# Rooms of two banks for the whole kernel: one PSUM pool, a gather with one eviction, taps in two transfers, and a new order of a gated mix of two long convolutions

## The chip, the cores and the metric
The kernel runs on one core of a Trainium2 chip. The metric is the device time of one launch in microseconds (us). The kernel before takes 266.55 us, the median of three runs from 265.99 to 267.28. On the core, TensorE (PE) multiplies matrices, with PEld for its weight loads; VectorE (DVE), ScalarE (ACT) and GpSimd (POOL) work on elements; SyncE (SP) issues most transfers, and ACT and POOL have DMA queues of their own. Matmuls write into PSUM, which this kernel divides into eight banks of 512 fp32 columns by 128 partitions; ACT or DVE copies or multiplies a result out of it ("evicts" it), and then its place is taken by another.

## The reference: what is computed
Length L is 2048, D is 448 channels, N is 256 complex modes per channel, and everything is bf16 from outside. Two long convolutions along the sequence are mixed by a gate.

```python
x = A_u                                             # [1, 2048, 448]
g = sigmoid((x * gate_w).sum(-1, keepdims=True))
# a: S4. A kernel made of 256 modes per channel, then a causal convolution
dt = exp(log_dt); logdA = dt * (A_re + 1j*A_im); dB = dt * (B_re + 1j*B_im)
K = einsum("dn,dnl,dn->dl", C, exp(logdA[:, :, None] * l), dB).real
a = irfft(rfft(u, 2L) * rfft(K, 2L))[:L] + u * Dskip
# b: H3. Four shifted taps of k, times v, a causal convolution, times q (here q = x)
kv = sum_t(k shifted by t * shift_k[:, ks - 1 - t]) * v
b = x * (irfft(rfft(kv, 2L) * rfft(ssm_k, 2L))[:L] + kv * ssm_D)
return g * a + (1 - g) * b
```

## The kernel before, in words
**Transforms as matmuls.** The 448 channels are cut into four column groups of 28 columns for each of the four partition groups (`NQG`, `NC`). Each convolution of a column group goes through the same stages, each a set of matmuls into PSUM and an eviction back to SBUF: `spread` (L328, PSUM tile `ps_c`, result `zs`), `transform` (`ps_2`, named `ps` in some rows), a product of two spectra on DVE (`products`), `stage_a` (`ps_a`, result `U`) and `stage_b` (`ps_b`, whose result is multiplied or copied into `ug` or `uu`). The "B" convolutions (H3) take the columns of `vt` and of `ssm_k`; the "A" convolutions (S4) take those of `uu` and of a kernel that has to be made first.

**Making the S4 kernel.** `Tables` (L555 on) turns the modes into tables of powers `ET` with exponentials and sines on ACT; the phases `ks_ph` and the real parts `ks_mag` come through matmuls that multiply by a diagonal matrix of dt (`ks_dt`) and through DVE. Exponential and sine need different function tables, so ACT loads a table (`ACT_TABLE_LOAD`) where it goes from one to the other. `KGen.block` (L464) does it in eight blocks of 14 columns: DVE builds the tables `kg_TQ`, `kg_P` and `kg_TP`, 224 small matmuls add up in the PSUM tile `pk`, and ACT evicts it as `kg_S`. `KGen.gather` (L511) then picks and shifts the pieces with small matmuls into `ps_g`, in two halves of 448 columns, each evicted with one copy into `kg_KT`; and `block` (L891) spreads these 14 columns into `zsK` (again `ps_c`). Two blocks make one column group.

**PSUM.** Pool `psum` (L722) has three shared rooms of two banks each: all stages take the next free one. Pool `psk` (L723) has two tiles of one bank: `pk` for the accumulation (L885), one buffer for the whole kernel, and `ps_g`, also one buffer, which `gather` takes twice per block and `spread` four times (groups of 4, 4, 4 and 2 columns) in the first six blocks. The spread of the last two blocks goes through shared rooms, in groups of 8 and 6. `evac` (L728) is a copy on ACT; `evac_two` (L731), used in the last block and at the end, alternates between ACT (even index) and DVE (odd).

**The opening.** Before the first spread of `vt`, the H3 input must be there: the four taps of `shift_k` come with four transfers on ACT's queue (L781–782) into `wraw`, DVE multiplies them with unit matrices into `diag` (the row `front<-scratch`, since `diag` lies in the tile `front`, L820–822), PE multiplies the transposed k with them (`ps_v`, L823–833), and DVE multiplies eight such tiles with v in place (`vt<-ps_v,vt`, L834–835). `ks_dt` is made from `ldt` by an exponential and a copy (L815–819).

**The order.** Nothing is issued when it is written. `Order` and `Listed` (L124–155) record each call with its number, and `issue` plays them back in the hand-written list `ORDER` (L42–112), with a dependency from each instruction to the one before it on the same engine. So the list fixes the order on every engine and DMA queue, and a tile's room is claimed in the order of the list too. All instructions show the line of the playback, L149; they are told apart by their tiles.

```python
for run in ORDER.split():
    a, _, b = run.partition("-")
    for f, args, kw in self.calls[int(a):int(b or a) + 1]:
        ins = f(*args, **kw)
```

**The end.** `step` (L955 on) interleaves the stages of one column group with block j of the S4 kernel for the next. After the last block come the half transforms and stages of the last group, whose two halves alternate evictions between ACT and DVE, and 16 output transfers.

Of the kernel before, what the change touches and what calls it, by code (L numbers as in the profile page):

```python
# [136 lines left out]
class Order:  # L137

    def __init__(self, tc):
        self.tc, self.calls = tc, []  # L140
        for e in ("vector", "scalar", "tensor", "gpsimd", "sync"):
            setattr(self, e, Listed(self.calls, getattr(tc.nc, e)))

    def issue(self):
        last, done = {}, 0
        for run in ORDER.split():
# [914 lines left out]
```

## Time and profile before
| | |
|---|---|
| runs | 266.55 us median (265.99 to 267.28, three runs) |
| profiled execution | 266.88 us, with a span of 264.8 us |
| DVE busy | 243.4 us (92%) |
| ACT busy | 226.8 us (86%) |
| PE busy, weight loads | 213.7 us (81%), 194.2 us (73%) |
| mean granted PE clock | 0.942 of full speed |
| HBM traffic | 7.95 MB read, 2.87 MB written |

The span runs from the first to the last instruction of the profiled execution; the time of the launch has 2.08 us more around it. "Busy" is the time in which an engine worked on at least one instruction, so the sum of single durations can be above it. A row of groups gives the engine, the operation, the result and its sources, the shape (partitions x elements, type), how often it occurs, the busy time, the mean duration of one in ns, and the idle time just before these instructions, with what ended most of it. A row of the timeline has the start, the length, and in brackets the idle time before. A row of stretches has the stretch, its length, the busy time (and number of instructions) of PE, PEld, DVE, ACT and POOL, the granted PE clock, the mean busy share of the DMA engines, and GB/s.

### The profile page before, as it was taken

Reading aid. Unit: us, or ns where it says so; the run is one execution under the profiler, and the core shown is the slowest. Engines: PE = TensorE matmul, PEld = TensorE weight load, DVE = VectorE, ACT = ScalarE, POOL = GpSimd, SP = SyncE. Lnnn points to the kernel's source line nnn. Section 1 sums busy time; section 2 is a strip of 40 time slices with the busy share of each in tenths; the row PEclk is TensorE's granted clock in tenths of the full one; section 3 lists DMA queues with packets and bytes.
Section 4 is the critical chain, followed back from the end, with each engine's and each line's share of the span. In section 5 each row is a group of like instructions: output and inputs, shape, how many; then the busy total and the mean of one; then the engine's idle time right before and its main releaser. Section 6 shows DMA issues by size and latency. Waiting matters only on the chain.

```text
span 264.8 us, 12775 instructions
## 1 busy us (share of the span) xinstructions
PE 213.7 (81%) x5786; PEld 194.2 (73%) x5786; DVE 243.4 (92%) x506; ACT 226.8 (86%) x375; POOL 11.8 (4%) x46
## 2 busy tenths in 40 slices
PE   1611849799799999999899898899979998989820
PEld 1501739788688889889788788889969888979720
DVE  6599999899999999999989999989999999989950
ACT  2998789997999999999999999999999999485400
POOL 8000000000000100010100100001000100000000
PEclk9999979999999869999999999999986999999955
DMA  7999669952833702045626230423240360600087
GB/s 153 218 189 192 104 134 203 176 83 32 158 72 72 159 4 57 4 80 119 109 51 141 41 92 2 90 56 73 50 97 2 72 144 2 144 5 2 2 158 122
DMA packets 57077, 24.27 MB, mean 92 GB/s; under 512 B 52032, under 2 KB 54720, under 8 KB 57024
## 3 DMA queue, kind: packets, MB, share of 16 engines
q1 hardware_dynamic: 50752, 19.34, 38.9%
q0 software_dynamic: 1008, 3.21, 6.6%
q10 hardware_dynamic: 5264, 0.92, 2.1%
q8 instruction: 45, 0.74, 1.2%
q14 instruction: 8, 0.07, 0.1%
HBM read 7.95 MB, written 2.87 MB: 41 GB/s over the span
## 4 chain that ended last, share of the span: by engine, by line
DVE 37%; ACT 35%; PE 16%; DMA 4%; issue 3%; SPq 0%; ACTq 0%; DVEq 0%
ACT zs L149 12%; ACT zsK L149 7%; ACT ET L149 6%; DVE kg_P L149 5%; PE ps_v L149 4%; ACT U L149 4%; DVE kg_TQ L149 3%; PE ps_b L149 3%; DVE kg_TP L149 3%; DVE ET L149 3%; PE ps_c L149 3%; DVE zsS L149 3%; DVE vt L149 3%; DVE zs L149 3%; DVE sb_G L149 2%
## 5 line engine op out<-in xcount | busy, mean ns | idle before, releaser
L149 ACT CAST zs<-ps 128x896 bf16<-128x896 f32 x48 | 43.8, 944 | 1.9 <-PE ps L149 1.9
L149 ACT CAST zs<-ps_c 128x1024 bf16<-128x1024 f32 (+1 forms) x48 | 44.0, 976 | 0.5 <-PE ps_c L149 0.4
L149 PEld LDWEIGHTS <-front 128*32 128x32 bf16 (+1 forms) x496 | 19.9, 160 | 27.8 <-issue 17.3
L149 PE MATMUL pk<-kg_TP,kg_TQ 128*32 128x32 bf16 x1792 | 35.4, 241 | 0.9 <-issue 0.7
L149 PEld LDWEIGHTS <-kg_TQ 128*32 128x32 bf16 x1792 | 31.8, 160 | 3.5 <-issue 0.9
L149 PEld LDWEIGHTS <-s_W 128*128 128x128 bf16 x544 | 27.9, 98 | 7.9 <-issue 4.5
L149 PE MATMUL ps_a<-sa_R,zs 128*128 128x128 bf16 x224 | 32.0, 231 | 1.2 <-DVE zs L149 0.7
L149 PE MATMUL ps_b<-U,sb_G 128*128 128x28 bf16 x1024 | 30.8, 178 | 2.6 <-DVE U L149 1.2
L149 ACT CAST U<-ps_a 128x1024 bf16<-128x1024 f32 (+1 forms) x30 | 27.9, 962 | 5.4 <-PE ps_a L149 5.4
L149 PEld LDWEIGHTS <-sb_G 128*128 128x128 bf16 x1024 | 28.7, 98 | 4.7 <-issue 1.9
L149 PE MATMUL ps_v<-front 128*32 128x336 bf16 (+3 forms) x448 | 17.3, 319 | 17.1 <-DVE sb_offs L149 6.9
L149 PE MATMUL ps_a<-sa_R,zsS 128*128 128x128 bf16 x224 | 31.1, 227 | 0.0
L149 PEld LDWEIGHTS <-zs 128*128 128x128 bf16 x224 | 29.0, 150 | 1.9 <-DVE zs L149 0.8
L149 PEld LDWEIGHTS <-zsS 128*128 128x128 bf16 x224 | 29.4, 152 | 0.7 <-DVE zsS L149 0.4
L149 PE MATMUL ps<-zs,s_W 128*128 128x112 bf16 x384 | 27.1, 215 | 3.0 <-ACT zs L149 2.5
L149 DVE TENSOR_TENSOR kg_TP<-kg_TP,ET 128x1792 bf16<-128x1792 bf16 x23 | 24.7, 1083 | 0.5 <-ACT ET L149 0.5
L149 DVE TENSOR_TENSOR kg_TQ<-kg_TQ,ET 128x896 bf16<-128x896 bf16 (+1 forms) x36 | 24.6, 720 | 0.0
L149 ACT ACTIVATE ET<-ks_ph 128x448 bf16<-128x448 int16 x40 | 22.6, 596 | 1.8 <-DVE ks_ph L149 1.7
L149 DVE TENSOR_TENSOR kg_P<-kg_TP,ET 128x1792 bf16<-128x1792 bf16 (+1 forms) x25 | 23.3, 934 | 0.1
L149 ACT ACT_TABLE_LOAD x15 | 19.2, 1283 | 2.0 <-issue 1.8
L149 PE MATMUL ps_c<-Wc,uu 128*64 128x128 bf16 x224 | 18.7, 290 | 0.4 <-ACT zsK L149 0.2
L149 PE MATMUL ps_c<-Wc,vt 128*64 128x128 bf16 x224 | 17.2, 289 | 1.2 <-ACT zs L149 1.2
(101 smaller groups left out, 424.7 us busy)
## 6 DMA issues: line engine op xcount, KB each, us to landing
zsS<-zs SPq DMA_DIRECT2D x16, 448.0 KB, 4.4
kg_TP<-kg_P POOLq DMA_DIRECT2D x7, 448.0 KB, 4.4
vt<-in_B_v_dram SPq DMA_DIRECT2D x4, 448.0 KB, 7.5
skraw<-in_B_ssm_k_dram SPq DMA_DIRECT2D x16, 112.0 KB, 3.4
uu<-in_A_u_dram SPq DMA_DIRECT2D x4, 448.0 KB, 7.1
ks_xf<-xfd SPq DMA_DIRECT2D x3, 336.0 KB, 3.1
out_dram<-vt SPq DMA_DIRECT2D x8, 112.0 KB, 4.4
out_dram<-vt ACTq DMA_DIRECT2D x8, 112.0 KB, 4.6
```

What stands on the lines that cost most here:

```text
L149: ins = f(*args, **kw)
```

## The change
- PSUM becomes one pool with four shared rooms of two banks. `psk` is gone: `pk` takes a shared room per block, of which it uses one bank, and `ps_g` takes one shared room of two banks per block.
- `gather` evicts once: both halves lie in the two banks of its room, and a single copy of 896 columns moves them into `kg_KT`. The copy's order runs through the columns of a tap, so consecutive results are written 128 bytes apart.
- The spread of every block goes through shared rooms in groups of 8 and 6 columns, as the last two blocks did.
- The taps come in two transfers instead of four: one for three groups of channels, and one for the fourth.
- `ORDER` is new from end to end. On ACT's queue both transfers of the taps stand ahead of the first table load; before, one did, and three stood behind an exponential that needs `ldt`. On SP's queue `A_re` is first, and all four transposes of k stand ahead of the four transfers of v; before, one of v was ahead of the last transpose. The order has 9 table loads instead of 15, the six fewer all in the opening.
- A list `TURNED` names 15 calls that change their engine when the list is played: 12 copies go from DVE to ACT and three from ACT to DVE. To ACT go four `kg_TP` copies 224 wide, two `kg_TQ` copies 448 wide, the copy of `gw`, that of dt (112 x 4), `gb`, two half-transform copies `zsK<-ps` 448 wide, and one `U` of 768 columns; to DVE go two `zs` spreads of 512 columns and one `zsK` of 1024.
- With all of it ACT has 372 recorded instructions instead of 390, DVE 498 instead of 508, and PE as many as before. 28 more tiles are claimed from the shared rooms, 213 instead of 185.

```diff
 ORDER = (
...
 )
+TURNED = (
+    "62 945 1091 1481 1503 2118 2948 2970 4623 4661 5088 5818 6522 6540 6604 "
+)
...
+    def turn(self):
+        for i in map(int, TURNED.split()):
+            f, args, kw = self.calls[i]
+            self.calls[i] = (self.tc.nc.vector.tensor_copy if f.__name__ == "copy" else self.tc.nc.scalar.copy, args, kw)
+
     def issue(self):
+        self.turn()
...
-        pt = self.pk[:, 0:448].rearrange("p (n b) -> p n b", b=32)
+        pt = self.psum.tile([P, 2, 512], f32, name="pk", tag="ps")[:, 0, 0:448].rearrange("p (n b) -> p n b", b=32)
...
         for r in range(8):
-            if r % 4 == 0:
-                pt = self.psk.tile([P, 512], f32, name="ps_g")
-            o = pt[:, (r % 4) * 112:(r % 4) * 112 + 112].rearrange("p (b n) -> p b n", b=8)
+            if r == 0:
+                pt = self.psum.tile([P, 2, 512], f32, name="ps_g", tag="ps")
+            o = pt[:, r // 4, (r % 4) * 112:(r % 4) * 112 + 112].rearrange("p (b n) -> p b n", b=8)
...
-            if r % 4 == 3:
-                evac(KT[:].rearrange("p n (b r) -> p n b r", r=8)[:, :, :, r - 3:r + 1], pt[:, 0:448].rearrange("p (r b n) -> p n b r", r=4, b=8), r // 4)
+        evac(KT[:].rearrange("p n (b f r) -> p f r b n", b=8, f=2), pt[:, :, 0:448].rearrange("p f (r b n) -> p f r b n", r=4, b=8))
...
-    psum = ctx.enter_context(tc.tile_pool(name="psum", bufs=3, space=PSUM))
-    psk = ctx.enter_context(tc.tile_pool(name="psk", bufs=1, space=PSUM))
+    psum = ctx.enter_context(tc.tile_pool(name="psum", bufs=4, space=PSUM))
...
-    for g in range(4):
-        nc.scalar.dma_start(wraw[:, g], B_shift_k[top(g):top(g) + P, :])
+    rows = B_shift_k[0:P, :]
+    nc.scalar.dma_start(wraw[:, 0:3], bass.AP(rows.tensor, rows.offset, [[4, P], [448, 3], [1, 4]]))
+    nc.scalar.dma_start(wraw[:, 3], B_shift_k[top(3):top(3) + P, :])
...
-    pk = psk.tile([P, 512], f32, name="pk")
...
-        if j >= NBLK - 2:
-            spread(nc, psum, WcK, KA[H], cols, [range(0, 8), range(8, 14)], ev, at=at)
-        else:
-            spread(nc, psk, WcK, KA[H], cols, [range(0, 4), range(4, 8), range(8, 12), range(12, 14)], evac, 4, "ps_g", at)
+        spread(nc, psum, WcK, KA[H], cols, [range(0, 8), range(8, 14)], ev, at=at)
```

More of the change, by code (lines that the diff above doesn't have):

```diff
@@ L406, with __init__ @@
 class KGen:
-    def __init__(self, tc, nc, pool, pk, psk, cons, sel_d, d4, EQ, EP):
-        self.tc, self.nc, self.pk, self.psk = tc, nc, pk, psk
+    def __init__(self, tc, nc, pool, psum, cons, sel_d, d4, EQ, EP):
+        self.tc, self.nc, self.psum = tc, nc, psum
         self.pool, self.cons, self.sel_d, self.d4, self.EQ, self.EP = pool, cons, sel_d, d4, EQ, EP
@@ L884, in body @@
     V.tensor_scalar(out=sel_d[:], in0=dj[:], scalar1=0.0, scalar2=None, op0=ALU.is_equal)
-    pk = psk.tile([P, 512], f32, name="pk")
-    kg = KGen(tc, nc, kgp, pk, psk, cons, sel_d, d4, EQ, EP)
+    kg = KGen(tc, nc, kgp, psum, cons, sel_d, d4, EQ, EP)
     KA = [None] * NQG
```

136 rows, old and new, of the table ORDER are left out of this document.

## The prediction
> **What bounds the kernel now.** I read the page's first part, then busy time by stretches, then the timeline of the opening and the groups by form, and last the waits. The page (engine, busy us, share of the span):
> ```profile
> PE 213.7 (81%) x5786; PEld 194.2 (73%) x5786; DVE 243.4 (92%) x506; ACT 226.8 (86%) x375; POOL 11.8 (4%) x46
> ```
> DVE is busiest, but 92% is a mean over unlike stages. The stretches (us; then PE, PEld, DVE, ACT, POOL busy):
> ```profile
> 0.00:48.95 48.95, 23.82 (x528) 20.87 (x529) 42.71 (x147) 38.73 (x67) 5.65 (x39) 0.97 0.98 171
> 48.95:100.00 51.05, 46.92 (x1082) 42.16 (x1084) 50.95 (x101) 48.86 (x78) 1.89 (x2) 0.93 0.50 89
> 100.00:160.00 60.00, 56.26 (x1633) 50.92 (x1628) 58.29 (x110) 59.29 (x105) 2.57 (x3) 1.00 0.38 77
> 160.00:220.00 60.00, 56.29 (x1536) 51.80 (x1533) 58.41 (x110) 59.50 (x101) 1.71 (x2) 0.94 0.30 65
> 220.00:255.40 35.40, 30.43 (x1042) 28.49 (x1034) 33.09 (x43) 20.45 (x28) 0.00 (x0) 0.94 0.20 43
> 255.40:264.80 9.40, 0.00 (x0) 0.00 (x0) 0.00 (x0) 0.00 (x0) 0.00 (x0) 0.50 0.86 143
> ```
> From 48.95 to 220 DVE has only 3.4 us of idle time and ACT 3.4: both are full, and neither helps alone. Idle DVE time sits in the opening (6.2 us) and the end (2.3), and 9.4 us at the end are output transfers. The opening (start, length, in brackets the idle time before and who ended it):
> ```profile
> 9.32 1.56 DVE L149 TENSOR_TENSOR front<-scratch 128x1344 bf16<-128x1344 bf16 x1 [3.12 <-DMA scratch<-in_B_shift_k_dram]
> ...
> 36.84 9.37 PE L149 MATMUL ps_v<-front 128*32 128x448 bf16 x263 [4.58 <-DVE vt L149]
> ...
> 47.87 1.09 DVE L149 TENSOR_TENSOR vt<-ps_v,vt 128x896 bf16<-128x896 f32 x1 [1.07 <-PE ps_v L149]
> ...
> 48.44 2.84 ACT L149 CAST zs<-ps_c 128x1024 bf16<-128x1024 f32 x3 [0.40 <-PE ps_c L149]
> ```
> DVE waits 3.12 us for the taps; PE, with three rooms full of ps_v, waits 4.58 us for DVE to empty one; the last vt product ends at 48.95, and ACT's first eviction of a spread starts at 48.44. There the full stage begins. The groups that the change touches (busy us, mean ns):
> ```profile
> L149 ACT ACT_TABLE_LOAD x15 | 19.2, 1283 | 2.0 <-issue 1.8
> L149 ACT CAST zsK<-ps_c 128x512 bf16<-128x512 f32 x18 | 11.6, 647 | 0.6 <-PE ps_b L149 0.4 <-PE ps_c L149 0.2
> L149 ACT CAST kg_KT<-ps_g 128x448 bf16<-128x448 f32 x15 | 8.4, 559 | 0.6 <-PE ps_g L149 0.4
> L149 ACT CAST kg_S<-pk 128x448 bf16<-128x448 f32 x8 | 4.4, 545 | 0.0
> L149 ACT CAST zsK<-ps_c 128x256 bf16<-128x256 f32 x6 | 2.5, 419 | 0.0
> L149 ACT CAST zsK<-ps_c 128x1024 bf16<-128x1024 f32 x2 | 2.1, 1034 | 0.5 <-PE ps_c L149 0.5
> ```
> And PE's waits for ACT, of which the first is the handing over of the single ps_g bank (us, times, longest):
> ```profile
> PE ps_c L149 <- ACT zsK L149: 2.8, 6, 1.1
> ```
>
> **The change part by part.** The sum is made against this execution: 266.88 us, a span of 264.8 and 2.08 around it; the median of the three runs is 266.55, 0.33 lower.
>
> *ACT's work.* The new list has 9 table loads instead of 15, all six fewer in the opening: -7.7 us (six of 1283 ns). Gathered taps: 15 copies of 559 ns (8.4) become 8 of 896 columns. Spread of a block: per block 3 x 647 + 419 = 2.36 becomes 1034 + 826 (the 768-column row) = 1.86; six blocks, and one 1024 copy that goes to DVE: -4.0. The other turned copies: two of 512 columns leave (-1.3); two of 448 (+1.1), one of 768 (+0.8) and nine small ones (four 224 wide at about 0.37, two 448 wide at 0.55, three of 0.2 to 0.37) come: +3.4. What shows no row is the 896-column gather copy, which writes each column 128 bytes from the last. Lower end 0.94 (the 896-column zs copy, 944 ns). Upper end 1.36: the 1024-column copy costs 1084, which is 0.23 over 0.833 ns a column, kg_S 0.17 over it; the 0.06 between them, if due wholly to its 128 jumps, is 0.47 ns a jump, and 896 jumps are 0.42. I take 1.0, since kg_KT today, with 112 jumps, is only 14 ns above kg_S, which reads 448 columns likewise. The Trainium skill (SBUF — State Buffer, section Door 1: The DMA port swizzle, its note on cachelines) says that an access that leaves its 16-byte line pays; kg_KT's 14 ns agree with a small price, and the rival below holds a large one.
>
> Rows overlap: ACT's groups add to 260.8 us against 226.8 busy, 0.09 an instruction; DVE's to 272.4 against 243.4, 0.057. With that, ACT falls by some 6.5 us in all, but from its first spread eviction to its end I add up 191.4 us in both orders (191.8 with the copy at 1.0): the gain is all in the opening, and the full stage gets +0.4.
>
> *DVE's work.* Off: kg_KT 0.62, four copies of 0.212, two of 0.272, 0.22, 0.27 and 0.30, two zsK of 0.62, a U of 0.95: 5.0. On: two of 512 and one of 1024 columns from PSUM, at 1.03 ns a column between the 448 row (0.62) and the 768 row (0.95): 2.6. Net -2.4, or -1.8 after the overlap: 0.8 before the last vt product, 1.0 behind it.
>
> *The opening.* ACT's queue now issues both tap transfers ahead of its first table load, at about 1.2 and 1.8 us, where the last three went out from 4.43 behind an activation that waits for ldt. At the 4.1 us that such a transfer takes here they land by 6, and DVE reaches the product at about 6.5: the 3.12 us go. The bounds are 3.12 and 0 (one transfer with three times the pieces may land later). What is late next is ks_dt, since the copy of dt passed to ACT: DVE waits some 0.65 us there. The SP queue now has all four k transposes ahead of vt, and A_re first; both orders put 14 transfers ahead of the last vt piece, issued until 24.07 and landing in 7.5, so about 31.6. By adding rows, DVE comes to its first vt product at 32.5 (35.70 before); PE needs four rooms x 56 x 40 ns = 9 us from k's landing near 21, so four are full by then. Room by room behind that, DVE waits 0.45 for ps_v and ends the last product at 41.9 of work + 1.0 start + 0.65 + 0.45 = 44.0: -5.0 against 48.95. Its bounds are 0 and -6.2 (all idle time). Here the cover is PE and DMA: if vt lands at 35.7, the latest that the trace permits, 3 us are gone. ACT's list reaches its first spread eviction at about 43.5: ks_ph waits for DVE at 40.0, then 0.59, a load 1.28, five short ones 1.5. So ACT follows DVE.
>
> *Rooms.* 28 more claims of a shared room (8 pk, 8 ps_g, 12 ps_c), and pk holds its room for about 6 us of PE's work, 4.1 its own. They replace six handovers of one bank per block by three rooms. Bounds: all 28 wait as PE waited for that bank, 2.8/6 = 0.47 each, less 3.0 us of waits that go: +10.2; or only the 3.0 go, a gain that can reach DVE. I take 0: PE's other waits for rooms are about 6 us in 171 claims, 0.04 each. In the last block one copy replaces two, between which ACT and DVE alternated: kg_S start to ps_c was 234.51 to 237.75, 3.2 us; now 0.53 + 1.28 of ps_g + 1.0 + gaps is 2.95. I put that at 0, as with 1.36 it is.
>
> *Sum.* -5.0 (opening) - 1.0 (DVE behind it) + 0.4 (ACT) = -5.6, the 5.7 us of later idle and the output unchanged: 266.88 - 5.6 = 261.3.
>
> **Rivals.**
> 1. *Rooms stop PE* (slower). pk's room and both full stages: if 18 of 28 claims wait 0.47, the gain is spent (18 x 0.47 - 3.0 = 5.5); with 20 to 28, 267.7 to 271.5, middle 269.5. For it: PE is already 94% busy from 100 to 220. Against: claims so far cost 0.04.
> 2. *The opening's cover is gone.* vt or the sines late by 2 to 3 us: 264.
> 3. *The gather copy pays for each jump.* 8 x 0.42 more on a full ACT, 3.4 us less 0.4 already counted: 264.3. kg_KT's 14 ns speak against it. This is the rule of the Trainium skill's note named above.
> 4. *The rooms help.* PE's 3.0 us of bank waits were holding DVE and ACT: 258.3.
> 5. *The loads were hidden anyway and nothing moves.* Against it: ACT, loads included, was busy 12.56 of the 13.05 us from 35.39 to 48.44, so its loads had no cover there; 266.
>
> **How the numbers follow.** Forecast 0.52 (259.5 to 263.5), rival 1 0.16, rival 2 0.12, rival 3 0.07, rival 4 0.07, rival 5 0.06. A measurement of this kernel tells about 0.5%, 1.3 us, from no change: faster is below 265.2, slower above 267.9. Faster: 0.52 + 0.12 + 0.07 + 0.07 less 0.03 of their upper tails = 0.75; same: 0.05 of rival 5, 0.02 of rival 1, 0.03 tails = 0.10; slower: the rest of rival 1 and a little of 5 = 0.15. The range from 257.8 to 267.5 leaves out about 0.05 below and 0.14 above.
>
> **What would show it.** Right: nine table loads; DVE's tap product near 7 with no wait on the transfer; the last vt product near 44; kg_KT x8 near 1.0; DVE and ACT each with under 5 us idle from there to 215; last DVE work near 250. Wrong: PE waits at pk, ps_g or ps_c ended by ACT that sum to over 8 us; vt waiting on DMA; kg_KT at 1.3 or more; a longer tail behind the last pk.

## The result, and the profile after
The changed kernel takes 289.79 us (median of four runs, 289.43 to 292.55) where the kernel before takes 266.27 on the same chip: a ratio of 1.0903 (95% interval 1.0826 to 1.0980), slower by 9%. 261.3 was forecast, with a range from 257.8 to 267.5. The profiled execution has a span of 290.2 us. Ratios, here and below, leave out executions that took over 1.5% longer than the fastest of their kernel.

The page of the changed kernel (engine, busy us, share of the span, instructions):
```profile
PE 219.7 (76%) x5786; PEld 202.6 (70%) x5786; DVE 241.0 (83%) x496; ACT 245.7 (85%) x359; POOL 12.0 (4%) x46
```
DVE has less work, as forecast (241.0 after 243.4). ACT has 18.9 us more, though it lost six table loads. The stretches of the changed kernel, cut at the end of the opening (stretch, length, then PE, PEld, DVE, ACT, POOL busy, clock, DMA share, GB/s):
```profile
0.00:44.18 44.18, 23.72 (x520) 20.42 (x520) 41.83 (x144) 29.70 (x60) 5.72 (x39) 0.96 1.01 179
44.18:100.00 55.82, 47.74 (x1140) 44.52 (x1141) 55.20 (x105) 54.97 (x87) 1.95 (x2) 0.94 0.49 88
100.00:160.00 60.00, 48.09 (x1355) 43.85 (x1356) 47.34 (x93) 55.41 (x75) 2.58 (x3) 0.87 0.38 72
160.00:220.00 60.00, 51.60 (x1377) 47.78 (x1376) 52.27 (x97) 59.48 (x87) 0.86 (x1) 0.88 0.21 48
220.00:280.80 60.80, 48.56 (x1406) 46.00 (x1402) 44.37 (x60) 46.16 (x54) 0.86 (x1) 0.83 0.23 48
280.80:290.20 9.40, 0.00 (x0) 0.00 (x0) 0.00 (x0) 0.00 (x0) 0.00 (x0) 0.50 0.83 150
```
The first two rows are what was forecast: the opening is over at 44.18, and to 100 us DVE has 0.6 us of idle time. From 100 on, where the S4 blocks come one after the other, DVE stands idle 7.7 to 16.4 us in each row and PE 8.4 to 12.2, while ACT is busy 55.4 and 59.5 us of 60 until 220. The opening in the timeline (start, length):
```profile
7.50 1.54 DVE L158 TENSOR_TENSOR front<-scratch 128x1344 bf16<-128x1344 bf16 x1
...
43.10 1.08 DVE L158 TENSOR_TENSOR vt<-ps_v,vt 128x896 bf16<-128x896 f32 x1
```
DVE no longer waits for the taps, and the last vt product ends at 44.18, forecast as 44.0. The groups that the change touches (busy us, mean ns, idle time before):
```profile
L158 ACT CAST kg_KT<-ps_g 128x896 bf16<-128x896 f32 x8 | 34.0, 4249 | 3.6 <-PE ps_g L158 3.6
L158 ACT ACT_TABLE_LOAD x9 | 11.5, 1283 | 2.4 <-issue 2.3
L158 ACT CAST zsK<-ps_c 128x1024 bf16<-128x1024 f32 x7 | 7.3, 1040 | 0.0
L158 ACT CAST zsK<-ps_c 128x768 bf16<-128x768 f32 x7 | 5.8, 833 | 0.0
L158 ACT CAST kg_S<-pk 128x448 bf16<-128x448 f32 x8 | 4.4, 549 | 1.4 <-PE pk L158 1.4
```
The first row is the result: the gather's one copy takes 4249 ns, where 1000 were taken and 1360 was the upper bound. The others have the forecast durations. PE's waits show who pays (us in total, times, longest):
```profile
PE ps_c L158 <- ACT kg_KT L158: 12.2, 4, 3.6
...
PE ps_a L158 <- ACT kg_KT L158: 5.6, 2, 2.9
...
PE pk L158 <- ACT kg_KT L158: 3.0, 1, 3.0
...
PE ps L158 <- ACT kg_KT L158: 2.7, 1, 2.7
```
23.5 us of PE's waits are ended by this one copy: PE waits in the spread that reads its result, and in work whose room is emptied by an eviction that queues behind it on ACT.

### The profile page after: what moved, and what is told of

Read it like the earlier page. It is cut to its first block, busy times and chain, and to the rows that moved or that the text cites. A ratio compares the mean times of both kernels' runs of the same rounds, so it can differ in the third digit from the quotient of the medians.

```text
span 290.2 us, 12757 instructions
## 1 busy us (share of the span) xinstructions
PE 219.7 (76%) x5786; PEld 202.6 (70%) x5786; DVE 241.0 (83%) x496; ACT 245.7 (85%) x359; POOL 12.0 (4%) x46
## 4 chain that ended last, share of the span: by engine, by line
ACT 43%; PE 26%; SPq 11%; DVE 7%; issue 7%; DMA 3%; ACTq 0%; DVEq 0%
ACT zs L158 15%; SPq L158 11%; ACT kg_KT L158 11%; PE ps_c L158 5%; PE pk L158 5%; ACT ET L158 5%; PE ps_a L158 5%; PE ps L158 5%; ACT U L158 5%; ACT zsK L158 3%; PE ps_b L158 3%; DVE vt L158 2%; PE ps_g L158 2%; DVE kg_TQ L158 2%; ACT L158 1%
## 5 line engine op out<-in xcount | busy, mean ns | idle before, releaser
L158 ACT CAST zs<-ps_c 128x1024 bf16<-128x1024 f32 (+1 forms) x46 | 42.7, 975 | 0.2 <-PE ps_c L158 0.2
L158 PE MATMUL ps_a<-sa_R,zs 128*128 128x128 bf16 x224 | 34.5, 243 | 7.4 <-ACT kg_KT L158 5.6
L158 PEld LDWEIGHTS <-s_W 128*128 128x128 bf16 x544 | 31.7, 108 | 12.0 <-issue 9.7
L158 ACT CAST kg_KT<-ps_g 128x896 bf16<-128x896 f32 x8 | 34.0, 4249 | 3.6 <-PE ps_g L158 3.6
L158 PE MATMUL ps_a<-sa_R,zsS 128*128 128x128 bf16 x224 | 34.0, 242 | 0.0
L158 PEld LDWEIGHTS <-zs 128*128 128x128 bf16 x224 | 30.6, 153 | 0.6
L158 PEld LDWEIGHTS <-sb_G 128*128 128x128 bf16 x1024 | 28.5, 98 | 3.3 <-issue 2.1
L158 ACT CAST U<-ps_a 128x1024 bf16<-128x1024 f32 (+2 forms) x31 | 28.5, 968 | 1.0 <-PE ps_a L158 1.0
L158 PE MATMUL ps_v<-front 128*32 128x224 bf16 (+3 forms) x448 | 17.7, 329 | 10.7 <-DMA front<-in_B_k_dram 5.6
L158 PE MATMUL ps_c<-WcK,kg_KT 128*64 128x128 bf16 x224 | 12.5, 265 | 12.3 <-ACT kg_KT L158 12.2
L158 DVE TENSOR_SCALAR ks_ph<-ks_xf 128x224 int32<-128x224 f32 x60 | 14.3, 266 | 7.5 <-ACT ET L158 5.1
```

## Experiments: the copy
Each ratio is to the kernel before on the same chip, with its 95% interval. What are called microseconds of a ratio are at 266.5 us for 1. The first two diffs are against the changed kernel; from the section on the rest of the forecast on, the changed kernel is the one with one copy along the taps, unless the text says otherwise. Diffs are shortened; `...` stands for lines left out.

**One copy, written in address order.**
```diff
-        evac(KT[:].rearrange("p n (b f r) -> p f r b n", b=8, f=2), pt[:, :, 0:448].rearrange("p f (r b n) -> p f r b n", r=4, b=8))
+        evac(KT[:].rearrange("p n (b f r) -> p n b f r", b=8, f=2), pt[:, :, 0:448].rearrange("p f (r b n) -> p n b f r", r=4, b=8))
```


> The changed kernel, with its one gathered copy turned round: it walks through the result in address order (column, block, tap), so it writes contiguously and reads PSUM with jumps. Theory W (each 2-byte result that is written 128 bytes from the last is paid): the copy falls from 4.25 us to about 1.0, and the time by 8 x 3.25 = 26.0 us where all of it was on the path: about 264, below the kernel before. Theory R (the price is that of reading two banks in one copy, or of a pattern of four dimensions): the copy stays above 3 us, and the time near 290. Theory S (the shared rooms stop PE, and the slow copy only stands where PE is late): the copy falls, the time stays above 270, and PE's waits for rooms are over 8 us.

Measured: ratio 0.9945 (0.9905 to 0.9985). The group in its profile:
```profile
L158 ACT CAST kg_KT<-ps_g 128x896 bf16<-128x896 f32 x8 | 7.3, 918 | 3.2 <-PE ps_g L158 3.2
```
The same 896 columns out of the same two banks, with four dimensions, read with jumps and written in a row: 918 ns. So the price is one of writing (theory W). 1.0903 - 0.9945 are 25.5 us, of 8 x 3.33 = 26.6 us of copy: nearly all of it was on the path. PE's wait for kg_KT falls from 23.5 us to 0.3, and PE's waits at pk, ps_g and ps_c that ACT ends come to some 4 us, the largest 3.0: theory S is out. The ten runs of this kernel lie as far apart as 263.14 and 267.85 us, and the medians of all runs, 266.87 against 267.16, would give 0.999, so its small gain over the kernel before is less sure than the interval says. The next run has the same gain with less spread.

**Two copies, as before, out of the shared room.**
```diff
-        evac(KT[:].rearrange("p n (b f r) -> p f r b n", b=8, f=2), pt[:, :, 0:448].rearrange("p f (r b n) -> p f r b n", r=4, b=8))
+        nc.both(lambda f: nc.tc.nc.scalar.copy(KT[:].rearrange("p n (b f r) -> p f n b r", b=8, f=2)[:, f], pt[:, f, 0:448].rearrange("p (r b n) -> p n b r", r=4, b=8)))   # for f = 0 and 1
```


> The changed kernel, with the gather evicted by two copies of 448 columns in the form of the kernel before, out of the two banks of the shared room; order, rooms, taps and turned copies stay. Theory W: each copy takes about 0.56 us as before, two of them 1.1, and the time is 8 x 0.1 = 1 us above the kernel with one copy along the taps: about 265. Theory S: above 270.

Measured: 0.9954 (0.9930 to 0.9978), with ten runs from 264.32 to 266.79 us; sixteen copies of 552 ns. One copy or two makes no difference that can be told: joining them saves 8 x 0.19 = 1.5 us of ACT's time, and none that the ratio shows.

**The far writes alone, in the kernel before.**
```diff
-evac(KT[:].rearrange("p n (b r) -> p n b r", r=8)[:, :, :, r - 3:r + 1], pt[:, 0:448].rearrange("p (r b n) -> p n b r", r=4, b=8), r // 4)
+evac(KT[:].rearrange("p n (b r) -> p r b n", r=8)[:, r - 3:r + 1], pt[:, 0:448].rearrange("p (r b n) -> p r b n", r=4, b=8), r // 4)
```


> The kernel before, with the loops of its two gather copies put into the order of the changed kernel (column innermost, so that each result is written 128 bytes from the last); nothing else. Theory W: at (4249 - 944) / 896 = 3.7 ns a jump each copy of 448 columns goes from 0.56 to about 2.2 us, 16 of them cost 26.5 us more, and the time is 285 to 293. Theory R (two banks, four dimensions): the copies stay near 0.56 and the time near 266.

Measured: 1.0998 (1.0959 to 1.1038), 26.6 us. Its groups:
```profile
L149 ACT CAST kg_KT<-ps_g 128x448 bf16<-128x448 f32 x15 | 33.6, 2241 | 0.1
L149 DVE CAST kg_KT<-ps_g 128x448 bf16<-128x448 f32 x1 | 2.2, 2156 | 4.2 <-PE ps_g L149 4.2
```
15 x 1.68 + 1.54 = 26.7 us more copy, 26.6 us more time. The order of a copy's loops alone makes the whole slowdown in the kernel before, and the one copy on DVE is as dear as those on ACT.

**A price list.** Only copies; all else of the computation is left out.


> Only copies, three times each, on ACT and then on DVE; all else of the computation is left out, and the output is zeros. 448 columns of fp32 in PSUM to bf16 in SBUF with results 1, 2, 4, 8, 16, 64 and 65 elements apart (s1 to s65), runs of 2, 4 and 8 results with 128 bytes from run to run (r2, r4, r8), fp32 results 64 bytes apart (f16), the two forms of the 896-column gather (kt, far writes; kc, contiguous writes), contiguous writes with jumping reads (pt), SBUF to SBUF contiguous (w1), with far writes (w64), and with far reads (z64). Theory W by the jump: s16 and s64 near 2.2 us on ACT and s1 near 0.55; r4 (112 jumps) near 0.55, as in the kernel before, r2 (224) in between, so that the price is not one per jump. Theory W by the multiple of 128 bytes: s65 as cheap as s1. Theory R: kt slow, s64 cheap.

In its groups, the two forms of the gather stand beside each other (a: ACT, v: DVE; kt: far writes, kc: in a row):
```profile
L63 ACT CAST akt<-src 128x896 bf16<-128x896 f32 x3 | 12.4, 4135 | 0.1
L63 DVE CAST vkt<-src 128x896 bf16<-128x896 f32 x3 | 12.4, 4131 | 0.1
...
L63 DVE CAST vkc<-src 128x896 bf16<-128x896 f32 x3 | 3.3, 1091 | 0.1
...
L63 ACT CAST akc<-src 128x896 bf16<-128x896 f32 x3 | 2.7, 905 | 0.1
```
The single durations from the trace, in ns, of 448 columns (the last of three):

| written | ACT | DVE |
|---|---|---|
| bf16 in a row (s1) | 532 | 626 |
| bf16, 4, 8, 16 bytes apart (s2, s4, s8) | 655, 1148, 2136 | 655, 1148, 2136 |
| bf16, 32, 128, 130 bytes apart (s16, s64, s65) | 2025, 2149, 2142 | 2026, 2148, 2142 |
| runs of 2, 4, 8 bf16, 128 bytes from run to run (r2, r4, r8) | 532, 532, 532 | 626, 624, 624 |
| fp32, 64 bytes apart (f16) | 905 | 904 |
| jumping reads, written in a row (pt) | 532 | 624 |
| out of SBUF, in a row and 128 bytes apart (w1, w64) | 564, 2182 | 276, 1199 |
| out of SBUF, read 128 bytes apart (z64) | 939 | 571 |

Out of PSUM, a lone bf16 result, 16 bytes or more from the last, costs (2136 - 532) / 448 = 3.6 ns more than one in a row on ACT, 3.4 on DVE. The 128 bytes have nothing to do with it (s65). And a jump is not what is paid: 224 jumps between pairs (r2), of which a part of the price was expected, cost nothing. Two bf16 results side by side are free here, 128 bytes from pair to pair; one alone is dear. Jumping reads are free out of PSUM (pt) only: out of SBUF they cost (939 - 564) / 448 = 0.8 ns each on ACT and 0.7 on DVE (z64), still less than lone writes there (3.6 and 2.1, w64).

## Experiments: the rest of the forecast
Without the price the change is worth 0.55%, 1.5 us (0.4 to 2.5), where 5.6 were forecast. What took the other 4?

**The taps.** Four transfers at the head of ACT's queue in the kernel before; and both behind the exponential (call 61) in the changed kernel:
```diff
 # before: order of the calls on ACT's queue
-0 22 ... 63 ... 25 ... 24 23
+0 22 23 24 25 ... 63
 # changed, one copy along the taps
-0 ... 22 ... 23 61
+0 ... 61 22 23
```


> The kernel before with one change of order: all four transfers of the taps stand together at the head of ACT's queue, ahead of the exponential that needs ldt. Theory O (DVE's 3.12 us wait for the taps was on the path of the whole opening and what comes earlier there ends earlier): the product of the taps starts near 6.5 us instead of 9.32, the last vt product moves from 48.95 to about 46, the time to about 264 (-1.1%). Theory H (hidden: PE, which waits for the transposed k, or the transfers of v set the end of the opening): the wait goes and the last vt product stays within 1 us of 48.95; no change in the time. Theory P (PE loses later what DVE wins in the opening): the last vt product is about 3 us earlier, the time less than 1.5 us.

> The changed kernel with one copy along the taps, and both transfers of the taps put behind the exponential of ldt on ACT's queue (about 4.7 us instead of 1.2). Theory O: DVE waits for the taps some 2 to 3 us again, the last vt product ends near 46.5 instead of 43.6 to 44.2, and the time is 2 to 3 us longer. Theory P: the opening is 2 to 3 us later and the time changes by less than 1.5 us, since DVE has time to spare in the last block (it was busy only 4.61 of the 10 us from 230 to 240). Theory H: nothing moves.

Measured: 0.9984 (0.9950 to 1.0017) and 1.0008 (0.9974 to 1.0042). The product of the taps in the two:
```profile
7.88 1.56 DVE L149 TENSOR_TENSOR front<-scratch 128x1344 bf16<-128x1344 bf16 x1 [0.55 <-DMA scratch<-in_B_shift_k_dram]
```
```profile
9.64 1.56 DVE L158 TENSOR_TENSOR front<-scratch 128x1344 bf16<-128x1344 bf16 x1 [2.06 <-DMA scratch<-in_B_shift_k_dram]
```
In the kernel before the wait falls from 3.12 to 0.55, but by the first vt product 0.38 us of that is left (35.32 after 35.70): hidden, theory H. In the new order the same wait, put back, makes everything some 2 us later in the profile, the first vt product (34.91 after 32.78), the last kg_S (237.51 after 235.77) and the end (span 265.4 after 263.5), as theory O has it. The ratios differ by 1.7 us (about 0.3 to 3.1), between the 2 to 3 of theory O and the less than 1.5 of theory P, so they alone do not decide. By the profile the opening's gain is not lost as such, and the taps bring it only together with the rest of the new order; which of its parts is needed was not taken apart.

**The rooms alone**, in the kernel before, with its order and its four groups of a spread. The lines that give `pk` and `ps_g` a shared room are left out.
```diff
-    psum = ctx.enter_context(tc.tile_pool(name="psum", bufs=3, space=PSUM))
-    psk = ctx.enter_context(tc.tile_pool(name="psk", bufs=1, space=PSUM))
+    psum = ctx.enter_context(tc.tile_pool(name="psum", bufs=4, space=PSUM))
...
-            spread(nc, psk, WcK, KA[H], cols, [range(0, 4), range(4, 8), range(8, 12), range(12, 14)], evac, 4, "ps_g", at)
+            spread(nc, psum, WcK, KA[H], cols, [range(0, 4), range(4, 8), range(8, 12), range(12, 14)], evac, at=at)
```


> The kernel before with the rooms of the change and nothing else: four shared rooms of two banks, pk and ps_g take one each per block, and each spread of a block goes through them in its four groups of 4, 4, 4 and 2 columns; order, evictions and their forms stay. It makes 40 more claims of shared rooms. Theory S (the rooms stop PE): waits of PE for evictions at pk, ps_g and ps_c grow by 5 us or more, and the time is 2 us or more longer. Theory N (rooms cost nothing, the one-bank handovers go): PE's wait at ps_c for zsK, 2.8 us, falls below 1, and the time is within 1 us or up to 3 us shorter.

Measured: 1.0043 (1.0024 to 1.0062), 1.1 us slower. PE's wait at ps_c for zsK falls from 2.8 to 1.9 only, and others come:
```profile
PE ps_c L149 <- ACT zsK L149: 1.9, 4, 0.9
PE ps L149 <- ACT zsK L149: 1.0, 2, 0.8
PE pk L149 <- ACT zsK L149: 0.7, 1, 0.7
PE ps_g L149 <- ACT kg_S L149: 0.7, 2, 0.3
PE ps_g L149 <- ACT kg_KT L149: 0.6, 2, 0.3
```
Neither theory came out. S is further off, with no growth of 5 us in those waits; but N's wait did not fall below 1, and the time is 1.1 us longer (0.6 to 1.7) where N allowed 1. That is some 0.03 us for each of the 40 more claims. Shared rooms are no gain and no disaster.

**The turned copies**: the list is emptied.
```diff
-    "62 945 1091 1481 1503 2118 2948 2970 4623 4661 5088 5818 6522 6540 6604 "
+    ""
```


> The changed kernel with one copy along the taps and an empty list of turned copies: 12 copies go back to DVE and three to ACT, in the places of the same order. DVE gets 5.0 us and gives 2.6, so it has 1.8 us more work after overlap. Theory D (DVE's work sets the pace behind the opening): 1 to 2.5 us longer than with the list. Theory P (DVE waits for PE in the last block anyway): within 1 us. The copy of dt goes back to DVE too, which alone changes nothing (below 0.3 us).

Measured: 1.0127 (1.0097 to 1.0158), 4.9 us longer than with the list, where DVE's work would give 1.8; both theories missed it. The last kg_S is only 0.2 us later (235.94), but DVE's last instruction ends at 257.71 instead of 253.96. Most of the list's worth is in the tail. With the list ACT does the last two evictions `U` one after the other, and DVE's products of stage_b begin at 249.45; without it two `zsK` and one `U` go back to DVE there, and the same products begin at 253.19:
```profile
246.61 1.75 ACT L158 CAST U<-ps_a 128x1024 bf16<-128x1024 f32 x2 [0.21 <-PE ps_a L158]
...
249.45 0.62 DVE L158 TENSOR_TENSOR ept<-ps_b,gt 128x448 bf16<-128x448 f32 x1
```
```profile
251.12 0.95 DVE L158 CAST U<-ps_a 128x768 bf16<-128x768 f32 x1
253.19 0.62 DVE L158 TENSOR_TENSOR ept<-ps_b,gt 128x448 bf16<-128x448 f32 x1 [1.13 <-PE ps_b L158]
```

**PE's standstills.** Where the copy is cheap, PE has waits that nothing in the profile ends ("issue"), in the kernel before first, in the changed kernel with one copy along the taps second:
```profile
PE ps_v L149 <- issue: 0.9, 1, 0.9
PE pk L149 <- issue: 0.7, 2, 0.4
PE ps_b L149 <- issue: 0.3, 1, 0.3
```
```profile
PE ps L158 <- issue: 4.3, 2, 3.2
PE pk L158 <- issue: 2.2, 2, 2.0
PE ps_c L158 <- issue: 1.3, 1, 1.3
PE ps_b L158 <- issue: 0.4, 2, 0.2
```
The longest, in its timeline, falls between two matmuls of one group, with all operands there:
```profile
140.45 0.42 PE L158 MATMUL ps<-zsK,s_W 128*128 128x112 bf16 x5
...
144.09 0.32 PE L158 MATMUL ps<-zsK,s_W 128*128 128x112 bf16 x3 [3.22 <-issue]
```
Numbered by PE's records in the trace (a weight load and a matmul count two, and each recorded wait between them one), the three longest standstills are ended by the instructions 4801, 5825 and 10177, and each of these leaves 193 modulo 256. (The expectations below use another count, in which the same three leave 211 to 221; only that the remainder is shared matters.) The page has 45 packets on a queue that carries instructions, and the 5786 weight loads and 5786 matmuls of PE make 257 for each:
```profile
q8 instruction: 45, 0.74, 1.2%
```
In the trace each of these packets has 16,384 bytes. So the guess was that PE stands at the end of a block of 256 instructions until the next is there. Six runs shift the ends of blocks against the work, by matmuls that nobody needs.

```diff
+        self.again(597, 65)      # one matmul of ps_m 64 times more
```


> The changed kernel with one copy along the taps, and one matmul of ps_m in the opening, where PE waits for k, done 64 times more; each later instruction of PE stands further back in its program. Nothing else changes. In the kernel without this PE stands still at 124.96, 144.09 and 229.72 us for 1.3, 3.2 and 2.0 us with no releaser in the profile, each time at the same place in a block of 256 of its instructions (the 211th to the 221st). Theory F (PE waits for its own next block of instructions): the three stalls leave these three matmuls and stand, where there are any, at other matmuls, again with one remainder modulo 256; the time may change by -3 to +2 us. Theory G (a wait at these matmuls that the profile doesn't show): the stalls stay at the same three matmuls.

```diff
+        nc.gpsimd.memset(z, 0.0)
...
+        for _ in range(n):       # ahead of PE's first instruction; n is 118, 66, 246 or 76
+            ins = nc.tensor.matmul(out[0:32, 0:32], lhsT=z, rhs=z, start=True, stop=True, tile_position=(0, 0))
```


> The changed kernel with one copy along the taps, and 118 matmuls of 32 columns on zeros at the very start of PE's list, where PE otherwise waits some 5 us for its first transfer; they push every later instruction of PE back by 236 places, that is, forward by 20 within its block of 256. Theory F (PE waits for its next block of instructions, and these waits cost time): PE's standstills at one remainder modulo 256, from 45 to 256 us, which sum to 11.2 us without this, fall to about 5 to 8 us, the opening is not later, and the time falls by 0.5 to 2 us. If the standstills fall and the time stays within 0.5 us, they cost nothing. Theory G: the standstills stay where they are.

> The kernel before, with 76 such matmuls at the start of PE's list: 152 places. Standstills of PE at block ends sum to 3.4 us in the kernel before; from the times at which PE gets through each block of 256 I work out that this shift puts the ends of blocks into the dense runs of pk and makes some 4 us more of them. Theory F: standstills of 6 to 10 us, all at one remainder, and the time 1 to 4 us longer. If the standstills come and the time stays within 0.5 us, they cost nothing.

> The changed kernel with one copy along the taps and 66 matmuls on zeros at PE's start instead of 118. Theory F (the place of the ends of PE's blocks of 256 instructions sets the price): the ends now lie where, by the times at which PE got through each block, 4 us more standstills arise than without filler; PE's standstills at block ends are 8 us or more, and the time is 1 to 5 us longer than with 118. Theory G (the filler as such helps: PE starts early): the time is within 0.7 us of that with 118, or in between.

> The same with 246 matmuls on zeros, 128 more than 118, that is, 256 instructions: the ends of blocks lie at the same matmuls. The filler ends near 7.7 us, up to 1 us behind the place where PE's first transfer ended its wait. Theory F: standstills at the same matmuls as with 118, about 5 us in sum, and the time that of 118 plus at most 1 us for the later start. Theory G: the time moves on with the filler, or the standstills stand elsewhere.

> The kernel before with 118 matmuls on zeros at PE's start. Theory F: the ends of blocks lie where I work out as few standstills as without filler (0.3 us against 0.3, where 76 gave 4.5); the time is within 1.5 us of the kernel before. Theory G (the filler as such costs the kernel before 9 us): 8 us or more longer.

Measured, with the standstills worked out from the starts of PE's weight loads in the trace (gaps above 0.4 us between 45 and 256 us whose end leaves 192 to 195 modulo 256; in brackets the two longest), and the end of the last vt product. This count gives 4.3 and 9.6 us where the expectations, by theirs, have 3.4 and 11.2:

| kernel | ratio (95%) | standstills, us | last vt product |
|---|---|---|---|
| before | 1 | 4.3 (1.4 at 47, 0.7 at 130) | 48.95 |
| before, 76 | 1.0328 (1.0295 to 1.0360) | 9.8 (3.0 at 90, 2.0 at 238) | 48.40 |
| before, 118 | 1.0003 (0.9977 to 1.0029) | 1.7 (1.2 at 148, 0.5 at 134) | 48.66 |
| changed, one copy | 0.9945 (0.9905 to 0.9985) | 9.6 (3.5 at 144, 2.2 at 230) | 43.59 |
| with ps_m 64 times more | 1.0060 (1.0027 to 1.0094) | 7.4 (2.8 at 194, 1.2 at 236) | 47.09 |
| 66 | 0.9968 (0.9940 to 0.9997) | 9.3 (2.9 at 192, 1.6 at 140) | 44.25 |
| 118 | 0.9858 (0.9811 to 0.9906) | 5.4 (2.1 at 226, 1.4 at 142) | 43.17 |
| 246 | 0.9932 (0.9908 to 0.9955) | 5.5 (2.5 at 230, 1.7 at 145) | 45.51 |

With 64 more of ps_m the three standstills are gone, and the longest, 2.8 us, is ended by instruction 8386, which leaves 194 modulo 256; without the 128 added instructions it is 8258, which leaves 66: theory F. Its time, 3.1 us longer where -3 to +2 was expected, says little, since the added matmuls delayed the opening by 3.5 us. The trace also shows what PE waits for: in all eight kernels, each of these standstills of over 1 us ends 1.2 to 1.7 us after the end of a packet on the instruction queue.

The filler at the start does not delay PE: it is idle there. 118 leaves 4.2 us fewer standstills and takes 2.3 us less time (0.6 to 4.0). 66, with half the filler, other ends of blocks and 3.9 us more standstills, takes 2.9 us longer than 118, 1.1 of them in the opening. 246, with the same ends as 118, has the same standstills; its 2.0 us more, where at most 1 was expected, are about the 2.3 us that its opening is later. In the kernel before, 118 changes nothing and 76 costs 8.7 us. So it is where the blocks end, not the filler.

What a standstill costs depends on where it falls, and that is not worked out. 118 takes 2.6 us of them out of the kernel before without a gain. Of the 8.7 us of 76 (1 to 4 were expected) 5.5 are new standstills, and the rest stays open; the granted clock is no cause that these runs show, since it was 0.932 in the mean of the runs with 76, and 0.927 with 118, which lost nothing. What makes a block late is not settled either: the packet with the block that PE awaited at 144.09 started at 141.4, 3.9 us after PE had passed the end of the block before, where 32 of 45 start within 1.5 us. The Trainium skill (Runtime: NRT & Kernel Launch, section Instruction fetch mechanics) has the blocks of 256 and calls the cost of crossing one mostly hidden; the blocks agree, but here up to 9.8 us were not hidden.

**pk first in the last block.** PE's order there, in words:
```diff
-pk x64, ps_2 (zsK) x32, pk x64 in pieces between them, ps_b x16, pk x64, ps_b x16, ps_a x12, kg_S, ps_g
+pk x224, kg_S, ps_2 (zsK) x32, ps_g, ps_b x32, ps_a x12
```


> The changed kernel with one copy along the taps; in the last block PE does all 224 matmuls of pk ahead of the half transform of zsK and of stage_b, then the gather's matmuls ahead of stage_b, and ACT evicts kg_S ahead of the four zsK. Theory L (the place of pk in PE's list of the last block gives the opening's gain back): kg_S starts at about 232.5 instead of 235.77 and the time falls by 1.5 to 3 us. Theory P (PE is behind with its work as a whole from 227 us on): kg_S starts earlier, what was put behind it ends later, and the time stays within 1 us.

Measured: 1.0023 (0.9992 to 1.0055), 2.1 us slower than without it, and kg_S starts at 235.40 instead of 235.77. Theory L falls, and P's 1 us is passed too. Its profile gives a part of why: the dense run of pk meets two ends of blocks, with standstills of 2.5 us at 230.46 and 1.7 at 234.19, both at 193 modulo 256; without the move the same two ends cost 2.2 and 0.5.
```profile
PE pk L158 <- issue: 3.7, 2, 2.3
PE ps L158 <- issue: 3.7, 2, 2.9
PE ps_c L158 <- issue: 1.5, 1, 1.5
```
The best kernel of all is the changed one with one copy along the taps and 118 matmuls of filler: 1.4% faster than the kernel before.

## Why the prediction was wrong, step by step
**The gather copy: the step that failed.** Some 25.5 of the 28.5 us between forecast and result are this copy. It was priced at 1.0 us between bounds of 0.94 and 1.36, and it takes 4.25. The upper bound made a price per jump out of the 1024-column copy (0.47 ns a jump) and took kg_KT's 112 jumps as evidence of a small one. Both write runs, of eight and of four results, and the price list shows that runs jump for free; the new copy's results stand alone, at 3.7 ns each ((4249 - 918) / 896). So the rows were near in shape and far in kind, and the bound was none. Rival 3 had the right mechanism, with a chance of 0.07 and an eighth of the price (3.4 us for 26.6). One row of the kernel before does write lone results, `skraw<-skraw,dB`, 28 columns 128 bytes apart on DVE: 276 ns, as long as a sum of 224 columns (`kg_TP<-kg_P`, 0.27 us). No price was taken from it. The Trainium skill's note (SBUF — State Buffer, section Door 1: The DMA port swizzle) spoke against the copy and gives no price; its line of 16 bytes agrees with the price list, where the cost stops growing at 16 bytes. Its two hits a line for full speed fit a pair (r2, 532 ns), but not two lone results in a line (s4, 1148).

**The opening: right, in its parts too.** Nine table loads, the tap product at 7.50 without a wait (forecast near 6.5), the last vt product at 44.18 (44.0), with DVE busy for 41.83 us of it (41.9) and idle for 2.35 (2.1). The cover that rival 2 doubted was there. But the taps were only part of its cause: alone they change nothing in the kernel before.

**DVE's work: right in size** (243.4 to 241.0, 2.4 less, where 1.8 were taken), too small in worth: the turned copies are good for 4.9 us, mostly in the tail, for which the sum had no term.

**Rooms at 0: nearly right.** They cost 1.1 us alone. Rival 1, the slower case with 0.16, had the sign of the result for a reason that did not come: its claims do not wait 0.47 us each. So the chance of 0.15 for a slower result came from a reason that did not hold.

**"The 5.7 us of later idle unchanged": failed, without the copy too.** With one copy along the taps the span is 263.5, the opening 5.4 us shorter and the end only 1.3 us earlier. In the stretch from 230 to 240 us DVE was busy 4.6 us of 10, where the kernel before had 9.2, with PE at 9.8: PE was late. The kernel before first, the one with one copy second:
```profile
230.00:240.00 10.00, 9.13 (x365) 8.32 (x356) 9.20 (x12) 6.62 (x10) 0.00 (x0) 1.00 0.07 16
```
```profile
230.00:240.00 10.00, 9.79 (x359) 9.01 (x351) 4.61 (x7) 4.22 (x7) 0.00 (x0) 0.83 0.02 5
```
The sum had no term for PE's standstills. 9.6 us of them at block ends in place of 4.3 are part of why, as far as the filler shows: 2.3 us of the missing 4.1 come back with 118. (The granted clock in the stretch is lower too, 0.83 after 1.00; with 118 it is 0.77 there, and that kernel is the faster.) With the 1.1 us of the rooms, if the two add up, 0.7 us are left without a cause. With intervals of 0.6 to 4.0 for the filler and 0.4 to 2.5 for the gain itself, this division is rough.

## What to carry to other kernels
Write the order of a copy's loops by its destination: bf16 results should land at least in pairs, and where the source is PSUM, jumps belong on the reading side. A row bounds a price only if it does the thing in question; where none does, look for the smallest instruction that does it (here 28 columns), or keep the range open. Where PE stands still with no releaser, number its instructions: if the remainders modulo 256 agree, a few idle matmuls at the start can be worth more than the change under study (here 2.3 us for 118 of them, after 1.5 for the change).

## What the runs showed of the hardware that was not expected
A lone bf16 result out of PSUM costs 3.6 ns more on ACT and 3.4 on DVE, from 16 bytes of distance on, and a pair costs nothing. 448 fp32 results 64 bytes apart take 905 ns, where as many bf16 results 32 bytes apart take 2025. A jumping read out of PSUM costs nothing; out of SBUF it costs 0.8 ns on ACT. PE stands up to 3.5 us at single ends of blocks of 256 instructions, until 1.2 to 1.7 us after the next block's packet of 16,384 bytes has ended, and 152 instructions more at the start of a program made a kernel of 266 us 8.7 us slower.
